# A fused kernel of linear attention and two feed-forward layers: block 0 takes all its units at once, the plan counts later DMAs longer, and three buffers are rearranged

## The chip, the cores and the metric

The kernel runs on one core of a Trainium2 chip. The metric is the device time of one execution in microseconds, the median of several runs. Engines are named as in the profile: PE (TensorE, matmuls) and PEld (its weight loads), DVE (VectorE), ACT (ScalarE), POOL (GpSimd), SP (SyncE, which issues nearly all DMAs).

## What is computed

Everything is in float32. First a linear attention with a decay per key dimension, over 4 x 8 heads, 768 positions and head size 48; then two feed-forward layers on the 3072 resulting tokens of width 384.

```python
def _attn_ref(q, k, v, alpha):
    for t in range(S):
        state = alpha[:, :, t, :, None] * state + np.einsum('bhd,bhe->bhde', k[:, :, t], v[:, :, t])
        y[:, :, t] = np.einsum('bhd,bhde->bhe', q[:, :, t], state)

def _moe_ref(x, w_a, w_b, w_out):          # 384 -> 1536 -> 384
    a = x @ w_a
    b = x @ w_b
    return a * b @ w_out

def _moe2_ref(x, w_in, w_out, alpha):      # 384 -> 2048 -> 384
    h = x @ w_in
    g = np.maximum(h, 0.0) + alpha * np.minimum(h, 0.0)
    return g @ w_out
```

## The kernel before

**Tiles.** The tokens are cut into 24 chunks of 128 positions of one batch entry; four chunks (one of each batch entry) are a block of 512 columns, so there are six blocks. A feed-forward unit is 256 columns of the hidden layer: six units in the first layer (each with three weights, wa, wb and wo) and eight in the second. Every operand of the feed-forward products is split into a high and a low part, and a product is three matmuls: high by high, low by high, high by low (`mm3`, L923 to L929). One step of PE is a group of nine matmuls: three pieces of the contraction (or three output banks) by three parts. `up` makes a group into one of two PSUM banks, `down` adds one into the three `acc` banks.

**Weights.** The first layer's weights arrive as float64 and are converted in the kernel (`conv`, L379 to L495): on DVE a first shift (L414), a shift of the raw word (L434), a merge (L438), a mask to the exponent (L450) and the low part (L453), with ACT before the first (L409) and before the last two (L446). Unit 0's three weights go another way, with PE (L481 to L483). The second layer's weights (`s`, from `rs`) are converted later, stored to DRAM (`w2d`) and loaded again (`v`).

**Attention.** For each chunk alpha is scanned twice on DVE: `scan_r` (L583) with the constant `ones`, whose head columns are 1, and `scan_a` (L592) with `invs`, whose head columns `recip` has filled. `mul` (L597) multiplies keys and queries (`kq`) by the scans. For blocks 0 and 1 PE transposes the keys; from block 2 on (`turned`) DVE turns 32 x 32 tiles (L660, into `kt`), four DMAs write them to DRAM (`ktd`, L664) and four read them back in the other order (`ks`, L674). `kt` and `ks` share one buffer. `pe_cross` makes the chunk's own scores by v and the state update; `mid` (L813) and `kept` (L816) add the state on DVE; `pe_own` finishes the output, and also makes the next chunk's scores, for which that chunk's `mul` must be done. ACT and DVE split the output into the high and low part of x (L876, L880). Six DMAs then move parts of x between partitions (L899); in block 1 they do so after each chunk.

**Order.** No engine's order is written out by hand. Every operation is added to a graph with its engine, a duration in ns, a key (when it is due), an added latency and what it waits for. `place` runs through time and lets each engine take the ready operation with the lowest key; `latest` turns the result into due times from the end; `search` (L288) tries 1500 random changes of the keys of what starts in the first 120 us and keeps the cheapest plan. The plan's order is then the order of the instructions on every engine, and the order of SP's DMA queue. Where the plan leaves PE idle for over 0.5 us before block 2, filler matmuls are put in (`fill`, L339).

**What sets the order here.** `SEGMENTS` says in which order blocks and units are due: block 0 with units 0 to 2, block 1 with units 0 to 2, block 0 with units 3 to 5, block 1 with units 3 to 5, then the other blocks with all six. A block that is interrupted leaves its three `acc` banks in SBUF (`part`, L993) and adds them later (L996). `SPLIT` names the (block, unit) pairs whose groups are cut into two halves of 256 columns, so that they can begin with two chunks. `place(g)` (L533) sets the key of a chunk's attention: 9.5 us apart in block 1, 12 us apart from block 2 on.

Of the kernel before, what the change touches and what calls it, by code (L numbers as in the profile page):

```python
# [25 lines left out]
P = 128  # L26
CH = 128
# [5 lines left out]

SEGMENTS = (
    (0, 0, 3), (1, 0, 3), (0, 3, 6), (1, 3, 6),
    (2, 0, 6), (3, 0, 6), (4, 0, 6), (5, 0, 6),
)
LAG = 2
SPLIT = ((0, 0), (1, 0))
BY_BLOCKS = 2  # L40

ON_PE = (("a", 0), ("b", 0), ("o", 0))
# [5 lines left out]
T_MOE = 30000  # L48
STRETCH = 1.2
URGENT = 40000  # L50
# [18 lines left out]
class Graph:  # L69
# [11 lines left out]
    def add(self, eng, dur, fn, key, deps=(), lat=0, after=(), pool=None, burst=False, line=None):  # L81
        o = Op()
        o.pool, o.hold, o.burst = pool, [], burst
        o.eng, o.dur, o.fn, o.key, o.lat = eng, dur - LEAD.get(eng, 0), fn, key, lat + LEAD.get(eng, 0)
        o.users, o.soft, o.n = [], [], len(self.ops)
        for d in {x.n: x for x in deps if x is not None}.values():
            d.users.append(o)
        for d in {x.n: x for x in after if x is not None}.values():
            d.soft.append(o)
        if line:  # L90
            if line in self.last and self.last[line] not in [x for x in after if x is not None]:
                self.last[line].soft.append(o)
            self.last[line] = o
        self.ops.append(o)
        return o
# [203 lines left out]
def body(tc, akq, v, vg, w_a, w_b, w_o1, w_in, w_o2, beta, out):  # L299
# [13 lines left out]
    with ExitStack() as ctx:  # L313
# [13 lines left out]
        betaT = const.tile([P, F2], F32, name="betaT")  # L327
        ones = pers.tile([P, NJ, CH + 1], F32, name="ones")
        invs = pers.tile([P, NJ, CH + 1], F32, name="invs")
        Z = pers.tile([P, BC, NJ, D], F32, name="Z")  # L330
        At = pers.tile([P, 2 * NC], F32, name="As")
        x2d = [dram.tile([P, 2, KT, MB], F32, name=f"x2d{n}") for n in range(NB)]
# [3 lines left out]

        warm = ones.bitcast(BF16)[:, 0, 2 : 2 + 2 * CH]

# [4 lines left out]

        nc.gpsimd.memset(ones, 0.0)
        nc.gpsimd.memset(ones[:, :, 0:1], 1.0)
        nc.gpsimd.memset(invs, 0.0)
        make_identity(nc, eye)
# [174 lines left out]
        xring, lring, rring, vring = Ring(2), Ring(2), Ring(2), Ring(2)  # L522
        aring, kring, sring = Ring(1), Ring(1), Ring(1)
        both = ps_att.tile([P, 2, 2 * NC // 2], F32, name="both")
# [4 lines left out]
        state = [[] for _ in range(BC)]  # L529
        sums = [At[:, NC + i * NJ * D : NC + (i + 1) * NJ * D].rearrange("p (j d) -> p j d", d=D) for i in range(2)]  # L530
        slots = [Z[:, c] for c in range(BC)] + sums[1:]

        def place(g):  # L533
            n, c = divmod(g, BC)
            key = c * 1000 - 100000 if n == 0 else block_at[n] - (BC - c) * 12000 - 14000
            if n == 1:
                key = block_at[n] - (BC - c) * 9500 - 6000

            def A(eng, dur, fn, deps, early=0, lat=0, after=(), line=None):
                return G.add(eng, dur, fn, key - early, deps, lat, after, burst=eng == "PE", line=line)  # L540

            return st[g], n, c, n == 0, A

        def inputs(g):
# [38 lines left out]
            def scan_r():  # L583
                nc.vector.tensor_tensor_scan(
                    out=s["ra"][:, 0 : NA - 1][:, ::-1], data0=s["ra"][:, : NA - 1 : -1],
                    data1=ones.rearrange("p j t -> p (j t)"), initial=0.0, op0=ALU.mult, op1=ALU.add,
                )

            def recip():
                nc.vector.reciprocal(invs[:, :, 0:1], r0())  # L590

            def scan_a():  # L592
                a = s["ra"][:, NA - 1 : 2 * NA - 2]
                nc.vector.tensor_tensor_scan(out=a, data0=a, data1=invs.rearrange("p j t -> p (j t)"),
                                             initial=0.0, op0=ALU.mult, op1=ALU.add)
# [4 lines left out]

            turned = n >= BY_BLOCKS
            r = A("DVE", 1220, scan_r, [la])
            rc = A("DVE", 180, recip, [r, before["scan"]])
            sa = before["scan"] = A("DVE", 1220, scan_a, [rc])
            slack = SLACK if not start else 0
# [35 lines left out]
        def chunk(g):  # L641
# [16 lines left out]
            def turn():  # L658
                s["kt"] = tp.tile([P, NJ, P], F32, name="kt", tag="ks", bufs=1)
                nc.vector.transpose(s["kt"], kT())  # L660

            def away(b):
                def f():
                    nc.sync.dma_start(  # L664
                        ktd[g].rearrange("t j a f -> t (j a) f")[:, :, b * SQ : (b + 1) * SQ],
                        s["kt"][b * SQ : (b + 1) * SQ].rearrange("p j (a d) -> p (j a) d", d=SQ),
                    )
# [9 lines left out]
            if turned:  # L677
                x = A("DVE", 650, turn, [k1, *kring.take()])
                lhold.append(x)
                moved = [A("SP", 430, away(b), [x], 0, 2000) for b in range(BT)]  # L680
                x = None
                back_at = []
                for a in range(BT):
                    x = A("SP", 350, back(a), moved, 0, 3800, after=[x])
                    back_at.append(x)
# [564 lines left out]
```

## Time and profile before

| | before |
|---|---|
| median of 3 runs | 942.45 us (941.32 to 942.47) |
| the profiled execution | 943.25 us |
| its span, first to last instruction | 941.5 us |
| PE busy | 932.5 us, 99% |
| PE weight loads busy | 760.1 us, 81% |
| DVE busy | 564.0 us, 60% |
| ACT busy | 245.2 us, 26% |
| moved by DMA | 112.89 MB |
| chain that ended last | PE 90%, DVE 5%, DMA 2% |

The page shows one profiled execution, so a sum worked out from its rows is compared with 943.25 us. A PE that is busy is not a PE at its peak, since matmuls are pipelined and their ends are modelled: the start of one group of matmuls to the start of the next tells how long a group takes, and a wait is shown in brackets behind the instruction that it ended with. Busy shares over the whole span hide that DVE is full in the first 120 us and half idle after that.

### The profile page before, as it was taken

How to read it: one execution, taken by the hardware profiler on the slowest of the kernel's cores; microseconds unless marked ns; L12 is line 12 of the kernel's file. 1: busy time of each engine (PE TensorE's matmuls, PEld its weight loads, DVE VectorE, ACT ScalarE, POOL GpSimd, SP SyncE). 2: the span in 40 equal slices, each digit the busy share in tenths (PEclk: the TensorE clock that was granted, in tenths of full speed). 3: DMA queues.
4: the chain of work that ended last, by engine and by line, in shares of the span. 5: the costliest groups of instructions: out<-in, count | busy, mean ns of one | idle time of the engine just before them, and what ended most of it. 6: DMA issues, size and time to landing. Idle time of an engine off the chain costs nothing.

```text
span 941.5 us, 15646 instructions
## 1 busy us (share of the span) xinstructions
PE 932.5 (99%) x6637; PEld 760.1 (81%) x6637; DVE 564.0 (60%) x865; ACT 245.2 (26%) x406; POOL 2.2 (0%) x11
## 2 busy tenths in 40 slices
PE   9999999999999999999999999999999999999998
PEld 7788887888888788787888888888888888888886
DVE  8999964674886687663232264554545545545554
ACT  3555531223333333331122121111111111111111
POOL 0000000000000000000000000000000000000000
PEclk9999999999999999999999999999999999999999
DMA  9973103563657767763266620100200200200000
GB/s 353 403 262 102 32 1 79 159 189 137 210 162 228 249 207 217 241 175 93 82 235 202 212 91 1 68 34 1 89 12 1 101 1 0 101 1 1 34 0 34
DMA packets 75238, 112.89 MB, mean 120 GB/s; under 512 B 38689, under 2 KB 48417, under 8 KB 75169
## 3 DMA queue, kind: packets, MB, share of 16 engines
q1 hardware_dynamic: 75024, 111.77, 36.1%
q8 instruction: 52, 0.85, 0.4%
q14 instruction: 18, 0.14, 0.0%
q10 hardware_dynamic: 144, 0.13, 0.0%
HBM read 78.97 MB, written 30.93 MB: 117 GB/s over the span
## 4 chain that ended last, share of the span: by engine, by line
PE 90%; DVE 5%; DMA 2%; issue 1%; SPq 1%; ACT 0%; DVEq 0%; ACTq 0%
PE acc L926 12%; PE acc L929 12%; PE acc L927 12%; PE pi L926 7%; PE pi L927 7%; PE pi L929 7%; PE pb L926 5%; PE pa L926 5%; PE pb L927 5%; PE pa L929 5%; PE pa L927 5%; PE pb L929 5%; PE both L786 2%; PE both L625 1%; DMA v<-in_v 1%; DMA ra<-in_akq 1%
## 5 line engine op out<-in xcount | busy, mean ns | idle before, releaser
L950 ACT CAST gh<-ng 128x512 fp32r<-128x512 f32 x96 | 59.5, 620 | 329.8 <-DVE ng L1163 274.0
L1159 DVE TENSOR_SCALAR ng<-pi,betaT 128x512 f32<-128x512 f32 x96 | 72.1, 751 | 105.6 <-PE pi L929 104.7
L954 DVE TENSOR_TENSOR gl<-ng,gh 128x512 fp32r<-128x512 f32 x96 | 66.3, 690 | 79.6 <-ACT gh L950 79.6
L926 PE MATMUL pi<-x,v 128*128 128x512 f32 x288 | 113.3, 393 | 0.0
L929 PE MATMUL acc<-gl,v 128*128 128x512 f32 x288 | 113.1, 393 | 0.0
L926 PE MATMUL acc<-gh,v 128*128 128x512 f32 x288 | 112.9, 392 | 0.0
L927 PE MATMUL pi<-x,v 128*128 128x512 f32 x288 | 112.7, 391 | 0.0
L927 PE MATMUL acc<-gh,v 128*128 128x512 f32 x288 | 112.1, 389 | 0.0
L1057 DVE TENSOR_TENSOR a_sb<-a_sb,pb 128x512 f32<-128x512 f32 (+1 forms) x76 | 49.9, 656 | 83.3 <-PE pb L929 83.3
L926 PE MATMUL pb<-x,wb 128*128 128x512 f32 (+1 forms) x228 | 87.8, 388 | 0.6 <-DVE a_sb L1057 0.6
L926 PE MATMUL acc<-gh,wo 128*128 128x512 f32 (+1 forms) x228 | 88.4, 388 | 0.0
L926 PE MATMUL pa<-x,wa 128*128 128x512 f32 (+1 forms) x228 | 87.3, 386 | 0.0
L929 PE MATMUL acc<-gl,wo 128*128 128x512 f32 (+1 forms) x228 | 86.8, 381 | 0.0
L927 PE MATMUL pb<-x,wb 128*128 128x512 f32 (+1 forms) x228 | 86.0, 380 | 0.5 <-DVE wb L453 0.5
L927 PE MATMUL acc<-gh,wo 128*128 128x512 f32 (+1 forms) x228 | 86.4, 379 | 0.0
L927 PE MATMUL pa<-x,wa 128*128 128x512 f32 (+1 forms) x228 | 85.9, 380 | 0.0
L950 ACT CAST gh<-a_sb 128x512 fp32r<-128x512 f32 (+1 forms) x76 | 45.3, 596 | 140.8 <-DVE a_sb L1057 131.5
L929 PE MATMUL pi<-x,v 128*128 128x512 f32 x288 | 81.6, 391 | 0.0
L1054 ACT COPY a_sb<-pa 128x512 f32<-128x512 f32 (+1 forms) x76 | 42.7, 562 | 107.1 <-PE pa L929 106.9
L1163 DVE SCALAR_TENSOR_TENSOR ng<-pi,ng 128x512 f32<-128x512 f32 x96 | 66.3, 691 | 3.1
L926 PEld LDWEIGHTS pi<-x,v 128*128 128x128 f32 x288 | 54.1, 188 | 13.7 <-DVE ng L1163 2.1
L954 DVE TENSOR_TENSOR gl<-a_sb,gh 128x512 fp32r<-128x512 f32 (+1 forms) x76 | 50.1, 659 | 25.0 <-ACT gh L950 24.9
(126 smaller groups left out, 1360.3 us busy)
## 6 DMA issues: line engine op xcount, KB each, us to landing
kq<-in_akq SPq DMA_DIRECT2D x24, 512.0 KB, 5.1
w2d<-ws SPq DMA_DIRECT2D x16, 768.0 KB, 5.1
v<-w2d SPq DMA_DIRECT2D x16, 768.0 KB, 5.9
x2d<-x SPq DMA_DIRECT2D x18, 512.0 KB, 3.7
x<-x2d SPq DMA_DIRECT2D x6, 1536.0 KB, 6.9
ra<-in_akq SPq DMA_DIRECT2D x24, 258.5 KB, 3.9
v<-in_v SPq DMA_DIRECT2D x24, 256.0 KB, 5.0
rs<-in_w_in SPq DMA_DIRECT2D x8, 768.0 KB, 6.0
```

The lines of the kernel that those rows point to most:

```text
L625: nc.tensor.matmul(a[hs, i, j, :], kT()[ps, j, hs], qT()[ps, j, hs], start=True, stop=True, skip_group_check=True)
L786: nc.tensor.matmul(y_of(k, half(p), part_of(h)), s["v"][part_of(h), 2 * j + i, :], s["As"][part_of(h), i, j, :], start=first, stop=False, ...
L926: nc.tensor.matmul(o, lh, rh, start=first and n == 0, stop=False)
L927: nc.tensor.matmul(o, ll, rh, start=False, stop=False)
L929: nc.tensor.matmul(o, lh, rl, start=False, stop=last and n == len(pairs) - 1)
L950: nc.scalar.copy(gq[idx][0], src())
L954: nc.vector.tensor_tensor(out=gl, in0=src(), in1=gh.bitcast(F32), op=ALU.subtract)
L1054: nc.scalar.copy(b["a"], ba["t"])
L1057: nc.vector.tensor_tensor(out=b["a"], in0=b["a"], in1=bb["t"], op=ALU.mult)
L1159: nc.vector.tensor_scalar(out=b["n"], in0=bh["t"], scalar1=0.0, scalar2=betaT[:, i : i + 1], op0=ALU.min, op1=ALU.mult)
L1163: nc.vector.scalar_tensor_tensor(out=b["n"], in0=bh["t"], scalar=0.0, in1=b["n"], op0=ALU.max, op1=ALU.add)
```

## The change

- The order of due work: block 0 passes all six units, then block 1, and so on. No block is interrupted, so no partial sums go through SBUF. Only block 0's unit 0 is cut in halves.
- The plan: chunks from block 2 on are due 16 us apart (`PACE`); every DMA that is due after 110 us is counted with 3.5 us more latency (`STEADY`, `SPARE`); the stretch of the due times is 1.1 in place of 1.2; the key writes and reads count 640 ns in place of 430 and 350, with 3.5 and 5 us of latency in place of 2 and 3.8.
- The turned keys `kt` get room behind the two state sums in `As`; the returned keys `ks` keep the old buffer. Turning a chunk's keys waits for the writes of the chunk before, no longer for its products.
- Both scans use one constant, `heads`. After `scan_a` POOL sets its head columns back to 1 (`begin`), and the next chunk's `scan_r` waits for that.

```diff
-SEGMENTS = (
-    (0, 0, 3), (1, 0, 3), (0, 3, 6), (1, 3, 6),
-    (2, 0, 6), (3, 0, 6), (4, 0, 6), (5, 0, 6),
-)
+SEGMENTS = tuple((n, 0, 6) for n in range(6))
 LAG = 2
-SPLIT = ((0, 0), (1, 0))
+SPLIT = ((0, 0),)
 BY_BLOCKS = 2
+PACE = 16000
+STEADY, SPARE = 110000, 3500
...
-STRETCH = 1.2
+STRETCH = 1.1
...
         o.pool, o.hold, o.burst = pool, [], burst
+        lat += SPARE if eng == "SP" and key > STEADY else 0
...
-        ones = pers.tile([P, NJ, CH + 1], F32, name="ones")
-        invs = pers.tile([P, NJ, CH + 1], F32, name="invs")
+        heads = pers.tile([P, NJ, CH + 1], F32, name="heads")
         Z = pers.tile([P, BC, NJ, D], F32, name="Z")
-        At = pers.tile([P, 2 * NC], F32, name="As")
+        At = pers.tile([P, NC + 2 * NJ * D + NC], F32, name="As")
...
-        nc.gpsimd.memset(ones, 0.0)
-        nc.gpsimd.memset(ones[:, :, 0:1], 1.0)
-        nc.gpsimd.memset(invs, 0.0)
+        nc.gpsimd.memset(heads, 0.0)
+        nc.gpsimd.memset(heads[:, :, 0:1], 1.0)
...
-        aring, kring, sring = Ring(1), Ring(1), Ring(1)
+        aring, kring, sring, tring = Ring(1), Ring(1), Ring(1), Ring(1)
...
+        kt = At[:, NC + 2 * NJ * D :].rearrange("p (j t) -> p j t", j=NJ)
...
-            key = c * 1000 - 100000 if n == 0 else block_at[n] - (BC - c) * 12000 - 14000
+            key = c * 1000 - 100000 if n == 0 else block_at[n] - (BC - c) * PACE - 14000
...
-                nc.vector.reciprocal(invs[:, :, 0:1], r0())
+                nc.vector.reciprocal(heads[:, :, 0:1], r0())
+
+            def begin():
+                nc.gpsimd.memset(heads[:, :, 0:1], 1.0)
...
-            r = A("DVE", 1220, scan_r, [la])
-            rc = A("DVE", 180, recip, [r, before["scan"]])
-            sa = before["scan"] = A("DVE", 1220, scan_a, [rc])
+            r = A("DVE", 1220, scan_r, [la, before["scan"]])
+            rc = A("DVE", 180, recip, [r])
+            sa = A("DVE", 1220, scan_a, [rc])
+            before["scan"] = A("POOL", 110, begin, [sa])
...
             def turn():
-                s["kt"] = tp.tile([P, NJ, P], F32, name="kt", tag="ks", bufs=1)
-                nc.vector.transpose(s["kt"], kT())
+                nc.vector.transpose(kt, kT())
...
             if turned:
-                x = A("DVE", 650, turn, [k1, *kring.take()])
+                x = A("DVE", 700, turn, [k1, *tring.take()])
                 lhold.append(x)
-                moved = [A("SP", 430, away(b), [x], 0, 2000) for b in range(BT)]
-                x = None
+                moved = [A("SP", 640, away(b), [x], 0, 3500) for b in range(BT)]
+                tring.use(*moved)
+                held, x = kring.take(), None
                 back_at = []
                 for a in range(BT):
-                    x = A("SP", 350, back(a), moved, 0, 3800, after=[x])
+                    x = A("SP", 640, back(a), [*moved, *held], 0, 5000, after=[x])
                     back_at.append(x)
```

The next six extracts show what the planner makes of that. Numbers behind names tell buffers apart; a line of the changed kernel is two or three above or below the old one.

DVE in the first block, before, the ten instructions up to number 181, which makes the low part of unit 4's wb (`c1`, `c2` are the conversion's work tiles, `ra` a chunk's alpha, `ro` a raw weight):

```order
L732 TENSOR_TENSOR As_97<-both_155,mask_92 128x512
L590 RECIPROCAL invs_95<-ra_1165 128x4
L414 TENSOR_SCALAR c1_1557<-c1_1557 128x768
L954 TENSOR_TENSOR gl_1572<-a_sb_1540,gh_1571 128x512
L594 SCALAR_TENSOR_TENSOR ra_1165<-ra_1165,invs_95 128x516
L434 TENSOR_SCALAR ro4_965<-ro4_965 128x768
L590 RECIPROCAL invs_95<-ra_1375 128x4
L450 TENSOR_SCALAR c1_1478<-c1_1478 128x768
L438 SCALAR_TENSOR_TENSOR c2_1558<-ro4_965 128x768
L453 SCALAR_TENSOR_TENSOR wb4_1545<-c2_1479,c1_1478 128x768
```

The same place in the changed kernel, up to number 190, which makes the low part of unit 5's wo, the last weight that block 0 needs:

```order
L662 STREAM_TRANSPOSE As_96<-kq_1343 128x512
L1060 TENSOR_TENSOR a_sb_1539<-a_sb_1539,pb_1542 128x512
L436 SCALAR_TENSOR_TENSOR c2_1471<-ro5_681 128x768
L957 TENSOR_TENSOR gl_1467<-a_sb_1433,gh_1466 128x512
L957 TENSOR_TENSOR gl_1578<-a_sb_1539,gh_1577 128x512
L819 TENSOR_TENSOR Z_95<-both_153,As_96 128x192
L448 TENSOR_SCALAR c1_1470<-c1_1470 128x768
L583 SCALAR_TENSOR_TENSOR ra_1404<-ra_1404,heads_94 128x516
L451 SCALAR_TENSOR_TENSOR wo5_1592<-c2_1471,c1_1470 128x768
```

All eighteen weights now stand in DVE's first 190 instructions; before, the first 181 held fourteen.

SP's DMA queue before, where the last chunk of block 1 is finished (the moves of `x_737` within SBUF) and the first turned chunk (`ktd8`) begins:

```order
L569 DMA v_1149<-in_v 128x512
L561 DMA ra_1165<-in_akq 128x517
L899 DMA x_737<-x_737 16x2x128 x6
L565 DMA kq_1316<-in_akq 128x1024
L569 DMA v_1332<-in_v 128x512
L899 DMA x_737<-x_737 16x2x128 x6
L561 DMA ra_1375<-in_akq 128x517
L664 DMA ktd8_128<-kt_1408 512x1x32 x4
L674 DMA ks_1473<-ktd8_128 32x4x128 x4
```

SP at the same place in the changed kernel:

```order
L560 DMA ra_1404<-in_akq 128x517
L564 DMA kq_1554<-in_akq 128x1024
L568 DMA v_1558<-in_v 128x512
L902 DMA x_960<-x_960 16x2x128 x2
L666 DMA ktd8_127<-As_96 512x1x32 x2
L902 DMA x_960<-x_960 16x2x128 x2
L666 DMA ktd8_127<-As_96 512x1x32
L902 DMA x_960<-x_960 16x2x128 x2
L666 DMA ktd8_127<-As_96 512x1x32
L560 DMA ra_1651<-in_akq 128x517
```

The six moves now stand with three of the four key writes of `ktd8` between them.

SP in the last block's attention, before: chunk 22's key writes and reads (`ktd22`, `ks_4754`), then chunk 23's load of keys and queries (`kq_4774`):

```order
L674 DMA ks_4592<-ktd21_141 32x4x128
L569 DMA v_4626<-in_v 128x512
L389 DMA rs1_4628<-in_w_o2 128x768
L1084 DMA w2d14_118<-ws0_4614 128x1536
L664 DMA ktd22_142<-kt_4689 512x1x32 x4
L674 DMA ks_4754<-ktd22_142 32x4x128 x4
L565 DMA kq_4774<-in_akq 128x1024
L569 DMA v_4778<-in_v 128x512
```

The same in the changed kernel, where chunk 23's load is `kq_4614`:

```order
L564 DMA kq_4457<-in_akq 128x1024
L1026 DMA x2d3_100<-x2_4440 256x1x512
L568 DMA v_4476<-in_v 128x512
L1026 DMA x2d3_100<-x2_4443 256x1x512
L1026 DMA x2d3_100<-x2_4523 256x1x512
L666 DMA ktd22_141<-As_96 512x1x32 x4
L564 DMA kq_4614<-in_akq 128x1024
L568 DMA v_4619<-in_v 128x512
L676 DMA ks_4654<-ktd22_141 32x4x128 x4
```

Chunk 23's load now stands between chunk 22's key writes and key reads.

## Rows read from the trace of the kernel before

**Rows 1.** the page, part 1: busy time of each engine, its share and instructions

```profile
PE 932.5 (99%) x6637; PEld 760.1 (81%) x6637; DVE 564.0 (60%) x865; ACT 245.2 (26%) x406; POOL 2.2 (0%) x11
```

**Rows 2.** PE's timeline: start, us, engine, line, operation, names, count [idle before]

```profile
47.68 0.28 PE L926 MATMUL pa<-x,wa 128*128 128x256 f32 x1
...
48.74 0.28 PE L926 MATMUL pb<-x,wb 128*128 128x256 f32 x1
...
58.06 0.50 PE L927 MATMUL pb<-x,wb 128*128 128x512 f32 x1 [0.55 <-DVE wb L453]
...
123.45 0.39 PE L926 MATMUL pa<-x,wa 128*128 128x512 f32 x1
...
125.51 0.39 PE L926 MATMUL pb<-x,wb 128*128 128x512 f32 x1
...
384.59 0.50 PE L926 MATMUL pb<-x,wb 128*128 128x512 f32 x1 [0.64 <-DVE a_sb L1057]
...
415.29 0.46 PE L786 MATMUL both<-As,v 64*64 64x64 f32 x16
...
430.25 0.46 PE L786 MATMUL both<-As,v 64*64 64x64 f32 x16 [2.03 <-DVE As L813]
```

**Rows 3.** the windows view, 0 to 110.31 us: PE, PEld, DVE, ACT, POOL busy (instructions)

```profile
0.00:110.31 110.31, 107.75 (x1271) 90.07 (x1272) 106.05 (x182) 53.92 (x98) 2.17 (x11) 1.00 0.66 243
```

**Rows 4.** DVE's groups by shape, 0 to 126 us: count | busy us, mean ns

```profile
L584 DVE TENSOR_TENSOR_SCAN ra<-ra,ones 128x516 f32<-128x516 f32 x12 | 14.6, 1224 | 3.6 <-DMA ra<-in_akq 3.6
...
L414 DVE TENSOR_SCALAR c<-c 128x768 uint32<-128x768 uint32 x16 | 8.9, 555 | 0.0
L450 DVE TENSOR_SCALAR c<-c 128x768 uint32<-128x768 uint32 x14 | 7.7, 553 | 0.0
...
L954 DVE TENSOR_TENSOR gl<-a_sb,gh 128x512 fp32r<-128x512 f32 x7 | 4.8, 686 | 0.0
...
L453 DVE SCALAR_TENSOR_TENSOR wa<-c,c 128x768 fp32r<-128x768 int32 x5 | 4.8, 958 | 0.0
L438 DVE SCALAR_TENSOR_TENSOR c<-ra 128x768 uint32<-128x768 uint32 x5 | 4.8, 958 | 0.0
...
L954 DVE TENSOR_TENSOR gl<-a_sb,gh 128x256 fp32r<-128x256 f32 x8 | 3.3, 418 | 0.0
...
L434 DVE TENSOR_SCALAR ra<-ra 128x768 uint32<-128x768 uint32 x5 | 2.8, 558 | 0.0
...
L690 DVE TENSOR_TENSOR Z<-Z,ra 128x192 f32<-128x192 f32 x7 | 2.5, 359 | 0.0
```

**Rows 5.** DVE's timeline, in the same columns as PE's

```profile
109.34 0.97 DVE L453 SCALAR_TENSOR_TENSOR wb<-c,c 128x768 fp32r<-128x768 int32 x1
...
419.85 0.56 DVE L450 TENSOR_SCALAR c<-c 128x768 uint32<-128x768 uint32 x1 [0.31 <-ACT ws L446]
...
427.51 1.22 DVE L599 TENSOR_TENSOR kq<-kq,ra 128x1024 f32<-128x1024 f32 x1 [4.30 <-DMA kq<-in_akq]
```

**Rows 6.** SP's DMA queue, timeline: start, time to issue, operation, count

```profile
45.51 4.77 SPq L899 DMA_DIRECT2D x<-x  x6
...
92.22 2.58 SPq L664 DMA_DIRECT2D ktd<-kt  x4
...
422.54 0.59 SPq L565 DMA_DIRECT2D kq<-in_akq  x1
```

**Rows 7.** DMA issues: count, KB each, median us from issue to landing

```profile
ktd<-kt SPq DMA_DIRECT2D x64, 64.0 KB, 3.4
...
x<-x SPq DMA_DIRECT2D x24, 16.0 KB, 2.7
```

**Rows 8.** ACT's groups by shape

```profile
L876 ACT CAST x<-both 128x512 fp32r<-128x512 f32 x20 | 11.6, 582 | 11.2 <-PE both L625 6.5 <-PE both L793 2.8 <-PE pb L929 1.5
```

**Rows 9.** ACT's timeline at 380 us

```profile
379.71 0.89 ACT L409 ACTIVATE c<-rs 128x768 f32<-128x768 f32 x1 [4.26 <-DMA rs<-in_w_in]
```

**Rows 10.** POOL's groups

```profile
L345 POOL MEMSET ones<- 128x4 f32 x1 | 0.1, 104 | 0.1
```

More of the change, by code (lines that the diff above doesn't have):

```diff
@@ L334, in body @@
         ktd = [dram.tile([SQ, NJ, BT, P], F32, name=f"ktd{g}") for g in range(NG)]
-        warm = ones.bitcast(BF16)[:, 0, 2 : 2 + 2 * CH]
+        warm = heads.bitcast(BF16)[:, 0, 2 : 2 + 2 * CH]
         def fill(t0, t1):
@@ L585, in scan_r @@
                     out=s["ra"][:, 0 : NA - 1][:, ::-1], data0=s["ra"][:, : NA - 1 : -1],
-                    data1=ones.rearrange("p j t -> p (j t)"), initial=0.0, op0=ALU.mult, op1=ALU.add,
+                    data1=heads.rearrange("p j t -> p (j t)"), initial=0.0, op0=ALU.mult, op1=ALU.add,
                 )
             def recip():
-                nc.vector.reciprocal(invs[:, :, 0:1], r0())
+                nc.vector.reciprocal(heads[:, :, 0:1], r0())
+            def begin():
+                nc.gpsimd.memset(heads[:, :, 0:1], 1.0)
             def scan_a():
                 a = s["ra"][:, NA - 1 : 2 * NA - 2]
-                nc.vector.tensor_tensor_scan(out=a, data0=a, data1=invs.rearrange("p j t -> p (j t)"),
+                nc.vector.tensor_tensor_scan(out=a, data0=a, data1=heads.rearrange("p j t -> p (j t)"),
                                              initial=0.0, op0=ALU.mult, op1=ALU.add)
@@ L665, in f @@
                         ktd[g].rearrange("t j a f -> t (j a) f")[:, :, b * SQ : (b + 1) * SQ],
-                        s["kt"][b * SQ : (b + 1) * SQ].rearrange("p j (a d) -> p (j a) d", d=SQ),
+                        kt[b * SQ : (b + 1) * SQ].rearrange("p j (a d) -> p (j a) d", d=SQ),
                     )
```

## The prediction, on record before the changed kernel ran

> **What bounds the kernel now.** I read first the busy times, then what PE itself waited for (its timeline), then the queues behind those waits. PE is busy in 99% of the span, DVE in 60%, ACT in 26% [rows 1]. A busy PE here means products end to end: a group of nine whole products (512 columns) takes 2.06 us from its start to the next group's (123.45 to 125.51), a group of nine half products (256 columns) 1.06 us (47.68 to 48.74) [rows 2]. So the time is PE's work plus the few places where PE stands still, and a change of order can win only there. Over the whole program PE's products before and after are the same but for the halves, so everything hangs on three things: stalls that go, stalls that come, and the halves.
>
> The stalls that I look at are 0.55 us at 58.06, where a product waits for the low half of a converted weight (unit 1's wb), 0.64 us at 384.59 for DVE, and 2.03 us at 430.25 for DVE's state update [rows 2]. Two other things bound stretches without showing as a PE wait. In the first 110 us DVE is saturated: 106.05 of 110.31 us busy in some 182 instructions [rows 3], so the order in which it converts weights sets when PE may go on. And SP's queue is in order: at 422.54 the load of a chunk's kq is issued only after the four key writes and four key reads of the chunk before it; DVE then stands 4.30 us for that load (427.51), and PE's 2.03 us follow from it [rows 5, 6].
>
> **The change, part by part.**
>
> *Halves.* Only block 0's first unit is still cut in two. Up to its first product of block 1 the new order has 261 whole and 108 half products, and every other PE item in the same number as the old order has when it first touches unit 3 (207 whole, 216 half), which is at 123.45 us [rows 2]. So 108 halves become 54 wholes: 12 x 1.06 - 6 x 2.06 = 0.36 us less. It also means that, with equal waits, PE comes to block 1 at 123.45 - 0.36 = 123.1 us. Two more fillers (81 for 79) stand where the plan expects PE to be idle: nothing.
>
> *Block 0 needs all six units at once.* This speaks against the change: DVE is full there. From the order, the last weight of block 0 (unit 5's wo) is DVE's 190th instruction; in the old order the 181st is unit 4's wb, which ends at 109.34 + 0.97 = 110.3 us [rows 5]. The difference between the two lists is three first shifts, three raw shifts and three merges (0.555, 0.558, 0.958), four exponent masks and four low parts (0.553, 0.958), less two scans (1.224 each), three state decays (0.359) and one masking as long as a whole low part (0.686), plus four whole low parts and four multiplies in place of as many halves (0.686 for 0.418, twice) [rows 4]: 6.21 + 6.04 - 2.45 - 1.08 - 0.69 + 2.14 = 10.2 us. Two reciprocals of four columns less are left out; the means count what neighbours overlap, so 10.2 is an upper figure. Unit 5's wo is ready at about 120.5 us, and PE wants it one group before block 1, at 123.1 - 2.06 = 121.0. It comes 0.5 us early: nothing, but the cover is thin. Earlier there is more: unit 1's wb is DVE's 80th instruction in place of its 92nd, while PE comes to it only two groups sooner, so the 0.55 us at 58.06 may go; I don't count it.
>
> *Block 1's start.* The last chunk of block 1 ends five whole groups before block 1's first product: 5 x 2.06 = 10.3 us. In that time come the ACT copy (0.582) [rows 8], the DVE split (0.686) [rows 4], and on SP six moves of x with three key writes between them, then the landing of the last. At the key writes' pace (2.58 / 4 = 0.645) nine issues take 5.8 us, at the moves' own (4.77 / 6 = 0.795) 6.7 us [rows 6]; the landing takes 2.7 or, as a key write, 3.4 us [rows 7]. That is 9.8 to 11.4 us: PE waits 0 to 1.1 us. The trace of before has no such mixture, and no end is nearer, so I take the middle, 0.6 us.
>
> *Longer DMAs in the plan.* The 0.64 us follow an ACT queue that stood 4.26 us for a late weight load (379.71) [rows 9]; the plan now adds 3.5 us to every DMA after its 110 us, and paces attention chunks at 16 us for 12. In the last block's attention, chunk 23's kq now stands ahead of chunk 22's key reads, and between the own parts of chunks 21 and 22 PE has ten groups in place of five: 20.6 for 10.3 us, against the 14.96 us from one part to the next that the trace needed with its stall (415.29 to 430.25) [rows 2]. Both stalls go: -0.64 and -2.03 us. If the cover were gone they would be back at those prices.
>
> *One constant for both scans.* Each scan of alpha now waits until POOL has set the four head columns back to one: 104 ns [rows 10], 24 times. The closest pair of scans has one kq multiply between them, which hides it: nothing.
>
> The Trainium skill, page "SBUF — State Buffer", section "Who interferes with whom", speaks against that: a GpSimd instruction and a VectorE instruction in a two-port mode lock each other out of a shared port for a whole instruction, and it lists tensor_scalar among those that can take that mode. No row here shows POOL and DVE at work together; by this rule a memset can wait for the conversions' shifts, or they for it (a rival below).
>
> *Keys in two buffers, no partial sums.* The turned keys no longer wait for the reading of the key buffer. Block 0 and block 1 no longer copy and add three partial banks each; the adds were DVE's, and the lists above contain that.
>
> Sum: -0.36 - 0.64 - 2.03 + 0.60 = -2.43 us. The profiled execution took 943.25 us, 0.8 above the median of 942.45; it would become 940.8, the median 940.0. A measurement of this kernel can tell about 0.2%, 1.9 us, from no change.
>
> **The rivals.**
>
> (A) *More goes.* Unit 1's wb is early, the 0.55 us go and block 1 starts without a wait: -3.6 us, 938.9. For: DVE's 80 in place of 92 instructions. Against: DVE is as full as before.
>
> (B) *The late stall stays*, because a DMA is late that the added 3.5 us don't cover, or because block 2's and later chunks meet another one of that size: 942.0. For: the 4.30 us wait is longer than 3.5. Against: ten groups in place of five.
>
> (C) *DVE falls behind in block 0: slower.* The 15 weights converted in the full way each cross to ACT and back twice. Here such a return left DVE idle 0.31 us where no other work stood ahead of it (419.85) [rows 5]. Thirty of them are 9.3 us; 0.5 are covered, so PE comes 8.8 us late to block 1, and the 0.6 us there vanish in it: 942.45 - 3.03 + 8.8 = 948.2. It decides from some 5.4 us of lost DVE time on: from there the kernel is slower by over 0.2%. For: DVE and PE now run in step for 120 us, where before DVE was ahead of PE from about 60 us on. Against: up to 58 us, where they were in step, the one recorded wait cost 0.55 us.
>
> (D) *POOL's memset locks with DVE.* Nine times in block 0 a scan waits for a shift (0.553) and the memset (0.104): 5.9 us, 5.4 beyond the cover: 942.45 - 3.03 + 5.4 = 944.8, slower. For: the two engines can meet there, and no row excludes it. Against: the order has at least one multiply between any two such scans, so nearly all of it would be hidden. It is what the page of the Trainium skill named above allows.
>
> **How the numbers follow.** Forecast 0.50; its own range is 938.4 to 941.2, from the wait of 0 to 1.1 us and the runs' own spread of about 1 us; some 0.37 of it is faster by over 0.2% (below 940.6), 0.13 within. (A) 0.14, faster. (B) 0.20, within 0.2%. (C) 0.13, (D) 0.03, slower; about half of (C) would be a smaller lag, between 944.3 and 946. So faster 0.51, same 0.33, slower 0.16. The range goes from 937.3, (A) with the runs' spread below it, to 944.3: it leaves out the slower cases and little else.
>
> **What would show it.** Right: PE's timeline has no wait of over 1 us after 130 us; block 1's first product starts near 123 to 124 us, with a wait of under 1.1 us for moves of x; unit 5's wo is done near 120 us; kq loads in the last block land before DVE asks for them; POOL's 24 memsets end before the scans want them. Wrong: PE standing still between 60 and 120 us for converted weights, DVE idle there for ACT or POOL, block 1 starting after 126 us, or a wait of 2 us in blocks 2 to 5.

## The result: slower by 1.2%, with the stalls gone

The changed kernel takes 954.03 us (median of 4 runs, 953.85 to 954.15), the kernel before beside it 942.46 (941.32 to 943.9): a ratio of 1.0122, 95% interval 1.0104 to 1.0139. 940.0 had been forecast, 944.3 at most, and none of the rivals reaches 954. The profiled execution's span is 952.3 us at a granted clock of 1.0, the 2.4 GHz level, as before.

The busy times of the changed kernel, then all that its PE waited for (engine, what it made and line, what it waited for; us in total, times, longest):

```profile
PE 946.2 (99%) x6585; PEld 755.7 (79%) x6585; DVE 561.1 (59%) x855; ACT 242.3 (25%) x396; POOL 6.9 (1%) x34
```

```profile
PE wp L341 <- POOL heads L343: 1.4, 1, 1.4
PE dS L761 <- DMA v<-in_v: 0.4, 1, 0.4
PE both L776 <- DVE x L883: 0.4, 1, 0.4
PE cl L479 <- ACT a_sb L1057: 0.2, 1, 0.2
```

The 0.55, 0.64 and 2.03 us of [rows 2] are gone, and what has come is 1.0 us in three waits (the 1.4 us are the start, before any data). So the order did what it was to do, and PE, with fewer waits, is busy for longer. The cause must lie in the products. PE's timeline of the changed kernel, at block 1's first product and at one place of the second layer (start, busy time, engine, line, tiles; the rows between are the other products of each group of nine):

```profile
123.52 0.39 PE L929 MATMUL pa<-x,wa 128*128 128x512 f32 x1
...
125.61 0.40 PE L929 MATMUL acc<-gh,wo 128*128 128x512 f32 x1
...
600.84 0.40 PE L929 MATMUL acc<-gh,v 128*128 128x512 f32 x1
...
602.94 0.39 PE L929 MATMUL pi<-x,v 128*128 128x512 f32 x1
```

A group of nine takes 2.09 to 2.10 us, from start to start; before it took 2.06 [rows 2]. The rows at 600 us lie in the second layer, whose products the change does not touch. Counted by the trace's groups of PE instructions there are 402 groups of nine whole products, 3618 products (the expectations below say 408 and 3672, six groups too many): with these rounded figures 402 x 0.04 = 16 us. PE's busy time says it more closely: 946.2 us against 932.5 [rows 1], 13.7 more. Against that stand 2.8 us fewer waits: 3.8 us have gone (the three above and two of 0.3 us shown further below), 1.0 us have come. 13.7 - 2.8 = 10.9, and the span grew from 941.5 to 952.3 us, by 10.8.

**What moved beside the order: addresses.** The constants, the state, x and the gated products lie behind each other in SBUF. One constant of 2064 bytes (laid out in 2080) went, the tile As grew by 1536: all that lies behind moved down by 544 bytes, which is 32 modulo 64. The places of the tiles in the two programs, in bytes from a partition's start (all weights lie 6144 bytes apart, a multiple of 256, so one stands for all):

```
              weights   x         gh        gl        modulo 64: weights, x, gh, gl
before        2752      136960    186112    192256    0,  0,  0,  0
changed       2752      136416    185568    191712    0, 32, 32, 32
```

### The profile page after: what moved, and what is told of

It reads as the page before. It is cut to its first block, busy times and chain, and to the rows that moved or that the text cites. A ratio compares the mean times of both kernels' runs of the same rounds, so it can differ in the third digit from the quotient of the medians.

```text
span 952.3 us, 15550 instructions
## 1 busy us (share of the span) xinstructions
PE 946.2 (99%) x6585; PEld 755.7 (79%) x6585; DVE 561.1 (59%) x855; ACT 242.3 (25%) x396; POOL 6.9 (1%) x34
## 4 chain that ended last, share of the span: by engine, by line
PE 98%; DMA 1%; DVE 0%; ACT 0%; issue 0%; POOL 0%; ACTq 0%; POOLq 0%
PE acc L929 13%; PE acc L932 12%; PE acc L930 12%; PE pi L929 7%; PE pi L930 7%; PE pi L932 7%; PE pa L929 6%; PE pb L929 5%; PE pa L932 5%; PE pa L930 5%; PE pb L932 5%; PE pb L930 5%; PE both L789 2%; PE both L628 1%; PE both L811 1%; PE wp L341 1%
## 5 line engine op out<-in xcount | busy, mean ns | idle before, releaser
L929 PE MATMUL pi<-x,v 128*128 128x512 f32 x288 | 114.3, 397 | 0.0
L930 PE MATMUL pi<-x,v 128*128 128x512 f32 x288 | 113.9, 395 | 0.0
L929 PE MATMUL acc<-gh,v 128*128 128x512 f32 x288 | 113.8, 395 | 0.0
L930 PE MATMUL acc<-gh,v 128*128 128x512 f32 x288 | 113.7, 395 | 0.0
L932 PE MATMUL pi<-x,v 128*128 128x512 f32 x288 | 82.7, 395 | 0.0
L932 PEld LDWEIGHTS acc<-gl,v 128*128 128x128 f32 x288 | 54.0, 187 | 13.2
```

The source lines that it names most:

```text
L929: nc.tensor.matmul(o, lh, rh, start=first and n == 0, stop=False)
L930: nc.tensor.matmul(o, ll, rh, start=False, stop=False)
L932: nc.tensor.matmul(o, lh, rl, start=False, stop=last and n == len(pairs) - 1)
```

## The experiments

A product has a loaded operand (here a slice of 128 columns of a weight) and a streamed one (512 columns of x, gh or gl). Both are fp32r, the type of the kernel's high and low parts; PE's rows call it f32. Two theories at first: *addresses* (a product is slower when an operand lies off a multiple of 64 bytes), and *order* (the new order, or POOL's 24 new instructions, slow the products). "Against" gives the kernel before, run beside each; the runs were made in several sessions, in which its own median lay between 942.3 and 943.4.

**32 bytes left free.** The order of every engine stays, to the instruction:

```
         heads = pers.tile([P, NJ, CH + 1], F32, name="heads")
+        pers.tile([P, 8], F32, name="pad")
```

> The changed kernel with 32 bytes per partition left free behind the one constant, and nothing else: the order of every engine is the same, and everything that lies behind it in SBUF (state, x, gates, the gated products gh and gl, attention's tiles) starts at a multiple of 64 bytes again, as before the change, and not 32 bytes past one. Theory (addresses): a group of nine products goes from 2.10 back to 2.06 us; 408 groups x 0.04 = 16.3 us, so 954.0 becomes about 937.7 (range 936 to 941). Rival (the new order, or POOL's new instructions, slow the products): nothing in the order moved, so 954 stays and groups stay at 2.10.

Measured: 939.38 us (939.17 to 939.51) against 943.42, ratio 0.9959 (0.9945 to 0.9972). 14.65 us came back by 32 unused bytes: 13.6 of PE's busy time (932.6 us on its page, 946.2 without the bytes) and the 1.0 us of waits. *Order* is out as the cause, and without the addresses the change gains 4.0 us here (2.6 in another session, see "Both edits").

**64 bytes left free**, the same edit with [P, 16].

> The same with 64 bytes left free: everything behind is moved by the same kind of edit, but starts 32 bytes past a multiple of 64 as in the changed kernel. Theory (addresses modulo 64): 954.0, groups of 2.10 us, no change to within 1 us. Rival (it is the distance between certain tiles, or any padding, that helps): near 938 as well.

Measured: 954.54 against 943.42. It isn't padding as such, nor that the tiles moved.

**The kernel before, with 32 bytes free** behind its tile `invs`.

> The kernel before with 32 bytes left free behind its two constants: old order, all tiles behind now 32 bytes past a multiple of 64. Theory (addresses): groups of 2.10 us, 942.5 + 16.3 = about 958.8 (range 956 to 960). Rival (order): 942.5, groups of 2.06.

Measured: 957.06 (955.68 to 958.75) against 943.42: 13.6 us slower in the old order too.

**32 bytes free ahead of the weights.**

```
         betaT = const.tile([P, F2], F32, name="betaT")
+        const.tile([P, 8], F32, name="pad")
```

> The changed kernel with the 32 bytes left free ahead of the weights: now all weights and the constant start 32 bytes past a multiple of 64, and x, gh, gl and all behind them at a multiple of 64. If the operand that streams through TensorE (the moving one) is what counts: as the 32 bytes behind the constant, about 937.7, groups of 2.06. If the operand that is loaded counts, or either one: groups of 2.10 or so, about 954. Rival (order): 954.

Measured: 953.95 against 943.42. Here x, gh and gl are at multiples of 64 and only the weights are not, and it is as slow. So it is not the streamed operand alone.

**Both edits.**

> The changed kernel with 32 bytes left free ahead of the weights and 32 behind the constant: weights, x, gh and gl all start 32 bytes past a multiple of 64. Shifting either of the two sides alone cost some 14.6 us (954.0 and 953.95 against 939.4). Theory 1 (only the two operands' distance modulo 64 counts): back to about 939.4, groups of nine at 2.06 us. Theory 2 (one operand off a multiple of 64 is enough, the second adds nothing): 954. Theory 3 (each costs by itself): 954 + 14.6 = about 969.

Measured: 939.64 (939.31 to 940.4) against 942.28, ratio 0.9969 (0.9958 to 0.9979). With everything 32 bytes off, nothing is lost: my theory of a multiple of 64 falls, and of theory 1 the distance stands (that it counts modulo 64 does not, as the tables show). The distances here are those of the kernel before, so this is a second measure of the change without the addresses: 2.6 us faster. What counts is the distance D from the loaded operand's address to the streamed one's.

**x alone and the gated products alone**, by a pad of 32 bytes in the pool between them (`cpool`), with and without the one behind `heads`.

> The changed kernel with 32 bytes free behind the constant and 32 more behind x: the state and x start at a multiple of 64, gh, gl and what lies behind them 32 bytes past one. Of some 408 groups of nine, 240 stream x and 168 stream gh and gl; 14.65 us over 408 groups are 0.036 us each. Theory (the products' own operands count, each group for itself): 954.0 - 240 x 0.036 = 945.4 (944 to 947), the first products' groups at 2.06 and the second products' at 2.10. Rival (it is another tile, the state or attention's or the gates', whose place slows everything): 939 or 954.

> The reverse: 32 bytes free behind x alone, so x stays 32 bytes past a multiple of 64, and gh, gl and attention's tiles start at one. Theory: 954.0 - 168 x 0.036 = 948.0 (946.5 to 949.5); first products' groups at 2.10, second products' at 2.06. Together with the reverse the two gains add up to 14.6. Rival: as in the reverse, 954 or 939.

Measured: 946.76 and 947.35 against 942.28; the gains of 7.27 and 6.68 us add up to 13.95 of the 14.65. PE's timeline with x alone at its old distance:

```profile
600.17 0.39 PE L931 MATMUL acc<-gh,v 128*128 128x512 f32 x1
...
602.27 0.39 PE L931 MATMUL pi<-x,v 128*128 128x512 f32 x1
...
604.34 0.39 PE L931 MATMUL acc<-gh,v 128*128 128x512 f32 x1
```

and with the gated products alone at theirs:

```profile
600.17 0.40 PE L930 MATMUL pi<-x,v 128*128 128x512 f32 x1
...
602.27 0.39 PE L930 MATMUL acc<-gh,v 128*128 128x512 f32 x1
...
604.33 0.40 PE L930 MATMUL pi<-x,v 128*128 128x512 f32 x1
```

In one program acc, which streams gh and gl, takes 2.10 and pi, which streams x, 2.07; in the other pi takes 2.10 and acc 2.06. Each product pays for its own two operands.

**A table of TensorE alone.** Groups of 72 products into one bank each; the loaded slice starts `wo` words, the streamed one `mo` words behind its tile's start.

```
+            for k in range(n):
+                c, r = s * wo + (k % 30) * P, s * mo + (k // 18 % 3) * MB
+                nc.tensor.matmul(t, w[:, c : c + P], m[:, r : r + MB], start=k == 0, stop=k == n - 1)
```

> No attention and no layers: TensorE alone runs groups of 72 products of 128 x 128 by 512 columns on zeros, each group with its own distance in bytes from a multiple of 64, of the loaded operand (0, 16, 32, 64) and of the streamed one (0 to 96 in steps of 8 or 16); then eight groups in bfloat16. It shows what one product takes at each pair. From the kernels: 228.5 ns at (0, 0), 233 at (0, 32) and (32, 0). Theory 1 (distance between the two modulo 64): (32, 32) as (0, 0), (0, 64) and (64, 0) too. Theory 2: (32, 32) at 233. Rival (the offset alone does nothing when nothing else runs; it takes DVE, ACT or DMA at the same SBUF to show): all groups alike.

PE's timeline. A name is the loaded operand's offset (wa 0, wc 16, we 32 bytes) and the streamed one's (ma 0, mb 8, mc 16, me 32, mf 40, mi 64, mm 96 bytes); hama and hamc are bfloat16. The two tiles lie 256 modulo 512 apart. The busy times are modelled ends: read from one start to the next.

```profile
31.06 16.48 PE L321 MATMUL wama<-M,W 128*128 128x512 f32 x72
47.38 17.00 PE L321 MATMUL wamb<-M,W 128*128 128x512 f32 x72
...
97.68 16.95 PE L321 MATMUL wame<-M,W 128*128 128x512 f32 x72
114.48 16.96 PE L321 MATMUL wamf<-M,W 128*128 128x512 f32 x72
...
164.83 16.64 PE L321 MATMUL wami<-M,W 128*128 128x512 f32 x72
181.31 16.97 PE L321 MATMUL wamm<-M,W 128*128 128x512 f32 x72
...
265.40 16.52 PE L321 MATMUL weme<-M,W 128*128 128x512 f32 x72
281.76 17.00 PE L321 MATMUL wemf<-M,W 128*128 128x512 f32 x72
...
382.15 16.72 PE L321 MATMUL wcmc<-M,W 128*128 128x512 f32 x72
398.72 16.61 PE L321 MATMUL wcme<-M,W 128*128 128x512 f32 x72
...
481.20 15.70 PE L321 MATMUL hamc<-M,W 128*128 128x512 bf16 x72
496.74 15.70 PE L321 MATMUL hame<-M,W 128*128 128x512 bf16 x72
```

A product takes 16.32 / 72 = 226.7 ns at the base, 16.80 / 72 = 233.3 with 32 bytes more, 16.48 / 72 = 228.9 with 64 more; with both moved by 32 it takes 16.36 / 72 = 227.2, as at the base. In these stretches DVE is busy for 0.00 us and the DMA share is 0.00, so it happens with the rest of the core idle: the rival falls. In bfloat16 all eight groups take 15.54 / 72 = 215.8. The surprise is that 64 more is not as good as the base; and with the loaded operand moved by 64 instead (415.16 to 431.96 us) a product takes 233.3, so theory 1's "modulo 64" falls. The rows with the loaded operand at 16 bytes speak against the distance alone: with both moved by 16 (wcmc) a product takes 16.57 / 72 = 230.1, not 226.7. So at steps of 16 bytes the places themselves count too; in the kernels all these tiles start at multiples of 32.

The Trainium skill, page "SBUF — State Buffer", section "Who interferes with whom", gives TensorE two read ports in SBUF, one for the moving operand and one for the load of weights, and calls them independent. By that rule D would not matter; the measured 6.6 ns between two distances say otherwise, for these fp32r products.

**The period.** A second table, D from 0 to 576 in steps of 64.

> A second table of TensorE alone, with the distance D (streamed operand's address less the loaded one's, in bytes, modulo 512) from 0 to 576 in steps of 64, then the same backwards, then some odd multiples of 32, then pairs moved together. From the first table (base distance 256 modulo 512): one product took 226.7 ns at the base, 228.9 at 64 more, 233.3 at 64 less and at any odd multiple of 32, 231.7 at 16 more; pairs moved together by 32 as the base (227.2). Theory (the load of the next weights and the streaming of this product's columns meet in SBUF, and how often depends on the distance modulo some power of two): a pattern in D that repeats, pairs moved together alike; if it repeats after 256: 226.7 at 0, 256, 512; 228.9 at 64, 320, 576; 233.3 at 192, 448. If after 128, the value at 64 less would have been that at 64 more, which the first table already excludes. Rival (absolute addresses decide): pairs moved together differ.

```profile
31.61 16.48 PE L321 MATMUL fara<-M,W 128*128 128x512 f32 x72
47.93 16.66 PE L321 MATMUL farb<-M,W 128*128 128x512 f32 x72
64.43 16.90 PE L321 MATMUL farc<-M,W 128*128 128x512 f32 x72
81.17 16.96 PE L321 MATMUL fard<-M,W 128*128 128x512 f32 x72
97.96 16.53 PE L321 MATMUL fare<-M,W 128*128 128x512 f32 x72
114.32 16.66 PE L321 MATMUL farf<-M,W 128*128 128x512 f32 x72
```

16.32, 16.50, 16.74, 16.79, then 16.36 and 16.50 again: it repeats after 256 bytes, at 226.7, 229.2, 232.5 and 233.2 ns for D = 0, 64, 128 and 192. Going the other way the order of the four is reversed, and the pairs moved together, here by multiples of 64, agree. With D modulo 256 all kernels fall into line:

```
kernel            D of x, of gh/gl   us
pad224            0, 0               932.99
before            64, 64             942.46  (old order)
pad32, both32     64, 64             939.38, 939.64
x_only            64, 96             946.76
g_only            32, 64             947.35
changed           32, 32             954.03
weights32         32, 32             953.95
pad64             96, 96             954.54
before_shift32    96, 96             957.06  (old order)
```

**D = 0 in the kernel**, 224 bytes ([P, 56]) behind `heads`. The kernel before has 128 bytes of SBUF left, so there it can't be had by a pad.

> The changed kernel with 224 bytes left free behind the constant in place of 32: x, gh and gl then lie 256 bytes modulo 512 from the weights, the base of the first table; with 32 bytes (as in the kernel before) the distance is 64. Theory (distance decides): 16.48 - 16.32 us for 72 products are 2.2 ns each; 3672 products x 2.2 = 8.2 us: 939.4 becomes about 931.2 (930 to 934), groups of nine near 2.04 us. Rival (any multiple of 64 is as good in the kernel, where DVE, ACT and DMA use SBUF too): 939.4.

Measured: 932.99 (932.49 to 933.12) against 942.3, ratio 0.9902 (0.9888 to 0.9915): faster than both kernels, by 9.3 and 21.0 us. The rival falls. PE's timeline:

```profile
600.97 0.39 PE L930 MATMUL acc<-gh,v 128*128 128x512 f32 x1
...
605.04 0.39 PE L930 MATMUL pi<-x,v 128*128 128x512 f32 x1
```

Two groups lie between, of 2.035 us each. The gain over D = 64 is 6.4 us, not the 8.2 expected: two waits of 0.4 us come with it, so the products gained 7.2. For the 3618 products that there are, the first table's 2.2 ns make 8.0 us and the second's 2.5 ns 9.0. Between D = 64 and 32 the kernel paid 13.6 us without the waits, against 15.9 by the first table (4.4 ns) and 14.8 by the second (4.1 ns). So the kernel pays eight to nine tenths of the table's price; where the rest goes was not tested.

**The size of load and stream.** A third table; `wc` columns loaded, `cols` streamed.

> A third table of TensorE alone, at the distances D = 0, 64, 128, 192 and 32: whole products (128 columns loaded, 512 streamed), then with 64 and with 32 columns loaded, then with 256 columns streamed, then with 64 loaded and 256 streamed. From the tables before, a whole product takes 226.7 ns at D = 0, 229.2 at 64, 232.5 at 128, 233.2 at 192 and 32, and in bfloat16, where half the bytes are read, 215.8 at every distance tried. Theory (the reads of the next load and of the running stream get in each other's way): with half the columns loaded, both what is over 215.8 at D = 0 (10.9 ns) and the spread over D (6.5 ns) halve (about 221 and 3 ns); with a quarter, 218.5 and 1.6; with 256 columns streamed and 128 loaded, the excess per product stays. Rival 1 (the start of a stream costs more at some addresses, whatever is loaded): excess and spread stay with fewer columns loaded. Rival 2 (every streamed column costs): with 256 columns streamed the excess halves, with fewer loaded it stays.

PE's timeline with half the columns loaded, at D = 0, 64 and 128:

```profile
114.76 16.73 PE L319 MATMUL halfloada<-M,W 128*64 128x512 f32 x72
131.32 16.61 PE L319 MATMUL halfloadb<-M,W 128*64 128x512 f32 x72
147.77 16.68 PE L319 MATMUL halfloadc<-M,W 128*64 128x512 f32 x72
```

From there to the next start 16.56 / 72 = 230.0 and 16.45 / 72 = 228.5 ns. All shapes so, in ns a product (columns loaded x streamed):

```
                D = 0    64     128    192    32     widest difference
128 x 512       226.7   229.2  232.4  233.3  233.2   6.6
 64 x 512       230.0   228.5  229.3  232.5  230.8   4.0
 32 x 512       231.5   231.7  230.8  231.5  233.2   2.4
128 x 256       119.9   117.9  118.6  113.8  116.7   6.1
 64 x 256       113.5   116.8  116.5  118.9   -      5.4
```

(No group starts after the last one, so the last row lacks D = 32.) No theory of mine fits. With 512 columns streamed the difference between distances shrinks with the columns loaded (6.6, 4.0, 2.4), as the theory said; with 256 streamed it hardly does (6.1, 5.4). With the stream halved it stays, so it is paid per product and not per streamed column. But the mean does not come down with the load, and the best distance is another for each shape: 0, 64, 128, 192, 0. What the load and the stream share is open; that the distance counts modulo 256 bytes for tiles at multiples of 32, and that D = 0 is best for whole products, is measured.

**Old order of block 0**, with the 32 bytes: only `SEGMENTS` and `SPLIT` put back.

> The changed kernel with 32 bytes free (939.4), and only the order of block 0 and block 1's first passes put back: three units of block 0, three of block 1, then the others; two halved units, partial sums in three banks. Theory (my sum's first term, and the wait of 0.5 us for unit 1's wb): halves +0.36 us, the wait +0.5: 939.8 to 940.3. Rival: the saturated DVE makes the new order of block 0 cost something that other parts cover: 938.5 or less.

Measured: 941.11 (940.9 to 942.0), 1.7 us above pad32's 939.38. Halves 0.36, and PE's waits (in pad32 only the start's remains):

```profile
PE both L632 <- DVE x L887: 0.5, 1, 0.5
PE wp L345 <- DVE a_sb L1064: 0.3, 1, 0.3
PE both L780 <- DVE As L735: 0.2, 1, 0.2
```

That is 1.4 of the 1.7. These rows are of its slowest execution, though, whose span is 2.4 us above that of pad32's profiled one (940.2 and 937.8): 1.0 us are the waits, and 1.4 are PE's busy time, 934.0 against 932.6, where the halves make 0.36. What the rest of the busy time is stays open. More than expected, same sign. The rival falls: in spite of DVE's load the new order costs less than the old one.

**Old figures of the plan**, with the 32 bytes:

```
-PACE = 16000
-STEADY, SPARE = 110000, 3500
+PACE = 12000
+STEADY, SPARE = 110000, 0
...
-STRETCH = 1.1
+STRETCH = 1.2
```

and the old costs of the turn and of the key moves.

> The changed kernel with 32 bytes free (939.4), and only the plan's figures put back: no 3.5 us added to late DMAs, chunks paced at 12 us, key moves costed as before, slack factor 1.2. The two key buffers, the one constant and the six-unit passes stay. Theory (the plan's figures removed the late stalls): waits of TensorE of 0.6 and 2.0 us in blocks 3 to 5 come back, 942.0. Rival (the second key buffer or the order of block 0 removed them): 939.4.

Measured: 945.62 (943.97 to 947.05), 6.2 us above pad32, more than twice what was expected. PE's waits:

```profile
PE both L790 <- DVE Z L820: 2.4, 1, 2.4
...
PE pb L930 <- DVE a_sb L1061: 0.8, 1, 0.8
PE kps L635 <- PE wp L342: 0.6, 1, 0.6
PE A L619 <- DVE As L732: 0.6, 1, 0.6
```

Stalls are back, but not where they were expected, in blocks 3 to 5: 2.4 us at 190.79, still among block 1's products, 0.8 soon after block 1's start (129.20), and 1.2 and 0.3 in the first 34 us. After 191 us PE waits for nothing. What does come back is the cause that the prediction named: DVE's waits for the loads of kq, first in the kernel before, then here; with 32 bytes free and the new figures there is one, of 0.5 us. The third row is the wait for the last chunk's kq, 4.30 us at 427.51 before [rows 5].

```profile
DVE kq L599 <- DMA kq<-in_akq: 27.4, 10, 5.4
...
DVE kq L602 <- DMA kq<-in_akq: 21.0, 10, 4.1
...
427.81 1.23 DVE L602 TENSOR_TENSOR kq<-kq,ra 128x1024 f32<-128x1024 f32 x1 [4.05 <-DMA kq<-in_akq]
```

So the plan's figures make the loads of kq early; where a late one reaches PE depends on the rest of the order. And the longest stall costs more than its length. PE around it, then the granted clock in windows of 2 us (window; sum, PE busy, PEclk, DMA share, GB/s):

```profile
190.79 0.46 PE L790 MATMUL both<-As,v 64*64 64x64 f32 x16 [2.42 <-DVE Z L820]
...
192.10 0.79 PE L930 MATMUL pa<-x,wa 128*128 128x512 f32 x1
...
195.81 0.40 PE L930 MATMUL pb<-x,wb 128*128 128x512 f32 x1
```

```profile
190.00:192.00 2.00, 1.21 (x80) 1.00 0.33 57
192.00:194.00 2.00, 2.00 (x17) 0.51 0.73 102
194.00:196.00 2.00, 2.00 (x7) 0.64 0.71 238
```

After PE had stood for 2.42 us its granted clock was 0.51, the 1.2 GHz level, from about 192 us on, and the products from 192.10 to 195.81 cost 1.65 us more than a group of 2.06. 2.4 + 0.8 + 0.3 + 1.2 + 1.65 = 6.35 us, of the 6.7 between this profiled execution (946.21) and pad32's. The clock seems not to fall in every execution: the four with a mean granted clock of 0.999 or 1.0 took 944.0 to 945.6 us, the six with 0.996 to 0.998 took 945.3 to 947.05.

Put back one at a time, the two parts cost 1.7 and 6.2 us, together more than the whole change gains without the addresses (2.6 to 4.0). So they hang on each other, and their prices cannot be added.

## Why the prediction was wrong

**The step that failed** is the first one, "Over the whole program PE's products before and after are the same but for the halves, so everything hangs on three things". Their number and order are; their duration is not, and I took 2.06 us a group as given. With it fails the sentence on the two key buffers and the one constant: I counted their instructions and never asked where the tiles then lie. The missing term is +14.65 us, shown by the 32 bytes; with it the forecast of 940.0 becomes 954.65, and 954.03 was measured. No rival had it, and none of the signs that I had listed under "Wrong" shows in the changed kernel's trace: PE does not stand still between 60 and 120 us, DVE is busy for 59.79 of these 60, block 1 starts at 123.52, and after it no wait is left. They all looked for waits and delays, and this loss is in products that run.

**The rest of the sum was right in sign, and in size as far as the runs can tell, but not term by term.** -2.43 us were forecast. With D put back the change gives 939.38 against 943.42, -4.0, and in the other session 939.64 against 942.28, -2.6: both the forecast and rival (A), -3.6, fit. Between the profiled executions' spans (941.5 and 937.8) it is -3.7, and the waits that went make up all of it: 0.64 + 2.03 + 0.55 + 0.30 + 0.25 = 3.77. By its terms:

- *Halves*: the -0.36 does not show. PE's busy time is 932.5 us before and 932.6 with 32 bytes free. Block 1's first product starts at 122.91 us there, against 123.45; but 1.1 us of waits before it have gone, and PE is busy for 121.33 us up to there, 120.89 before. The two more fillers, which I put at nothing, may cover it (the fillers are busy 12.6 us for 11.7); that was not tested. With only the order put back, PE is busy 1.4 us longer, so the order's own price is not settled by these runs.
- *The late stalls* of 0.64 and 2.03 us: gone, as forecast. For the second the chain is shown: the wait for the last chunk's kq goes with the new figures of the plan and comes back with the old ones. That these figures alone keep PE from standing there is not shown, since with the old ones it stands elsewhere.
- *0.55 us at 58.06*: gone, not counted by me. So are two waits of 0.3 us that I had passed over (rows of PE's waits in the kernel before):

```profile
PE cl L481 <- DVE a_sb L1057: 0.3, 1, 0.3
PE both L625 <- DVE x L880: 0.3, 1, 0.3
```

- *Block 1's start*: I gave 0.6 us for the moves of x; PE does not wait there.
- *(B)*, the late stall stays: fell. *(C)*, DVE falls behind: fell; block 0's last weight was forecast for 120.5 us, and DVE has written it at 119.27 + 0.94 = 120.2 (here with the 32 bytes):

```profile
119.27 0.94 DVE L452 SCALAR_TENSOR_TENSOR wo<-c,c 128x768 fp32r<-128x768 int32 x1
```

- *(D)*, POOL locks with DVE: the mechanism is there, its price is not. In the changed kernel, around two of DVE's shifts:

```profile
265.28 0.53 DVE L412 TENSOR_SCALAR c<-c 128x768 uint32<-128x768 uint32 x1
...
265.42 0.91 POOL L592 MEMSET heads<- 128x4 f32 x1 [18.67 <-DVE ra L596]
265.73 0.56 DVE L432 TENSOR_SCALAR rs<-rs 128x768 uint32<-128x768 uint32 x1
```

The memset, which takes 0.10 or 0.11 us in 17 of its 24 places, takes 0.91 here and ends at 266.33, when both shifts are done (266.29). By the Trainium skill, page "SBUF — State Buffer", section "Who interferes with whom", a GpSimd instruction and a VectorE instruction in a two-port mode, which tensor_scalar can take, lock each other out for a whole instruction, and the trace agrees. The 24 memsets take 0.22 us in the mean; in the kernel with 32 bytes free PE waits for nothing after its start, so they delay nothing that ends the run.

## What to carry to other kernels

In a program laid out like this one, an edit that adds, drops or resizes a tile moves all that is laid out behind it: compare the tiles' addresses of both programs, and the duration of one unchanged group of products, before reading a slowdown into the order. For the fp32r products of 128 x 128 by 512 here, with tiles at multiples of 32 bytes, the distance of streamed and loaded operand modulo 256 bytes is worth up to 2.9% of a product (226.7 to 233.3 ns); choose it by a pad, and measure it anew for another shape, since the best distance moves. A stall on a saturated TensorE can cost more than its length, when the clock falls after it (1.65 us here after one of 2.42).

## What was not expected of the hardware

- A product's time depends on D modulo 256 bytes: 226.7 to 233.3 ns for whole fp32r products on tiles at multiples of 32 bytes; in bfloat16 215.8 at all eight pairs tried (no pair there has D = 128 or 192).
- The clock fell after 2.42 us of standing still (granted 0.51, the 1.2 GHz level) and cost 1.65 us beyond them. In the profiled execution of the kernel before the granted clock stays at 1.00 in spite of the 2.03 us [rows 2]. Why runs of that kernel lie between 940.1 and 945.4 us, and those of the kernel with 32 bytes free between 939.2 and 939.5, is open: of its seven runs above 944 us three have a mean granted clock of 0.998, and four of 1.000.
